# Joining 16-blocks of a batch element's triangular inverses in 64x64 tiles, two 32-blocks to a product, and a new order of all steps

## The chip, the cores and the metric

One Trainium2 chip, of which the kernel uses one core. The metric is device time in microseconds (us) from launch to end. The kernel before ran at a median of 657.1 us over 3 runs (648.14 to 662.64). Engines: PE is the matrix engine (products), PEld its loading of weights, DVE, ACT and POOL the vector, scalar and general engines, SP the engine that issues all DMAs here. Every fp32 product is shown in the profile as two records of a weight load and a matmul, so the counts of records are twice those of products.

## The reference, cut to what matters

```python
# q, k, v: (4, 8, 768, 48); beta: (4, 8, 768)
k_n = k / (norm(k) + 1e-6)
for t in range(768):
    y[:, :, t] = q[:, :, t] @ state
    v_old = state^T k_n[t]
    state = state + beta[t] * outer(k_n[t], v[t] - v_old)
x = y with the 8 heads side by side: (4, 768, 384)
h = relu(x^T @ w_tok1) @ w_tok2          # tokens mixed: 768 -> 256 -> 768
u = x + h^T
out = u + relu(u @ w_ch1) @ w_ch2        # channels mixed: 384 -> 1536 -> 384
```

## The kernel before, in words

The recurrence over 768 tokens is done in chunks of 64 tokens. A unit u is a pair of chunks (128 tokens) of one batch element with all 8 heads; there are 24 units, six to an element. For each of 16 (chunk, head) blocks of a unit the kernel forms the strictly triangular 64x64 matrix of products of keys, and needs the inverse of one plus that matrix. With the inverses there, a chunk is one step of a chain over chunks: the state is multiplied with the chunk's keys and queries (`p_k`, `p_y`), the rest of the values with the inverse (`p_w`), and the state is updated (`p_s`).

All engines take their instructions in program order. The program is a set of Python generators ("jobs"), each cut into steps by `yield`, and a string written out in the source, `order` (lines 1124 to 1193), names which job does its next step; every engine and the DMA queue on SP gets its instructions in that order. The jobs:

- `k<u>` loads keys and queries, `v<u>` values (line 406), `w<j>` one piece of the weights (`round_weights`, line 262): step 0 is the DMA on SP (line 271), step 1 two ACT passes (277, 278), step 2 a DVE pass (280), step 3 a POOL pass (284). The buffer of a piece, `d64`, has three copies, so the DMA of a piece waits for step 3 of the piece three before it in the order.
- `p<u>` prepares a unit: transposes of keys and queries (463, 481), products `p_g` (501), masked copies by DVE (507), and then `to_parts` (567): for the six units of the first element the four 32x32 diagonal blocks go to the tile `spare` by copies of ACT (572), DVE (575) and POOL (577); later units go by DMA to DRAM (584).
- `i<r>` inverts the 32x32 blocks of a round of units in DVE (`invert`, 615). The first element has the rounds 0 (units 0 to 3) and 1 (units 4, 5). For these two the elimination (637, 642) inverts two 16x16 diagonal blocks of each 32-block side by side in 14 steps, and step 15 writes a transposed copy `t16` of the upper 16 rows (651). Step 16 transposes the inverses back (654).
- `h<u>` (`join_16`, 661), first element only, fills the 16x16 off-diagonal block of each 32-block: per (chunk, head) block and per quarter of 32 partitions, one product with the 32-block as weights and 16 columns of `t16` (672), an ACT copy that keeps the lower 16 rows by a scale `low16` (675), one product of that with the 16 right columns of the 32-block (682), and four ACT copies into place (687). A unit has 32 products of each kind: 8 pairs of blocks times 4 quarters.
- `f<u>` (589) brings the inverted 32-blocks back, `j<u>` (694) joins two 32-blocks to a 64-block (`p_z` 715, `p_x` 718 and 734).
- `r<t>` (740) is the chain over the 48 chunks, 12 to an element. `m<b>` (943) is the whole mixer of element b: token mixing (950, 963), then the channel mixing (1030 or 922, then 1052). Its first `p_h` (963) needs all 12 chunks of its element.
- `x`, `z` (221) and `Y` (230) are fillers: products of zeros into a tile `p_warm` that nobody reads. `x` is a 128x128 product with 128 columns, `z` one with 512 columns (both line 225), `Y` four of 64x64 with 128 columns (235).

Tiles in PSUM of the names `p_z`, `p_x` and `p_g` share two buffers, tag "prep".

Of the kernel before, what the change touches and what calls it, by code (L numbers as in the profile page):

```python
# [23 lines left out]
def kernel(  # L24
# [402 lines left out]
    def gm_of(u):  # L427
        return gms[place(u)]
# [113 lines left out]
    )  # L542

# [71 lines left out]
    def invert(rnd):  # L615
# [45 lines left out]
    def join_16(u):  # L661
# [4 lines left out]
        bs = slice(j * NB, j * NB + NB)  # L666
        z = z16[:, bs]
        p_z = ps_prep([128, NB, QB], "p_z")
        for nb in range(NB):
            for i, (block, _, _) in enumerate(quarters(u)):  # L670
                r = slice(HB * i, HB * i + HB)
                nc.tensor.matmul(p_z[r, nb], block[:, nb], t16[r, :, j * NB + nb])
        taken_16.add(u)
        yield
        nc.scalar.activation(z, p_z, ACTF.Copy, scale=low16)
        yield
        assert inverted.issuperset((u, i) for i in range(4))
        p_x = ps_prep([128, NB, QB], "p_x")
        for nb in range(NB):
            for i, (block, _, _) in enumerate(quarters(u)):  # L680
                r = slice(HB * i, HB * i + HB)
                nc.tensor.matmul(
                    p_x[HB * i : HB * i + QB, nb], z[r, nb], block[:, nb, QB:HB]
                )
# [440 lines left out]
    x z w10 b*2 w10 k1 k0 k1*5 k0*2 w2 w1 w10*2 p1*2 k3 k0*3 z p0 p1 b p0*3 p1*2 p0*6  # L1125
    w2 p0 k2 p0 w1 k3 w2 w3 k3 p0 k2 k4*2 k3 p1*4 w1 p1 w1 p1 k4*2 k2 x k3 p0 z p1 p0
    k4 p1 k5*2 k2*3 p2*2 v0*2 w3*3 p2 k3 p3 p2 p3 p2*4 k5 p2*2 p3 p4 w13 p1 w18 z w2 p0
    p3*2 v0 p2 p3 v1 p2*2 p3*3 k5*2 k6 p2 p3 p4 k4 p3*3 p4 w13 w6 p2*2 p1*2 p3*2 k5 p4
    w13 k7*2 p3 i0*6 p5 i0*2 w6 p4*3 k6 p4 i0*4 k6 p4*2 i0*2 k6 i0 p4 w18 k6 z w18*2 i0
    p4*3 p5*2 v1 w13 Y h1*2 h0 i0 k7*2 p6*2 f0*2 w8 w17 f0 h2 h0*2 w8 f1 p5 k7 h0*2 p6  # L1130
    h0*2 h2 p5 v0 w17 f1*2 p7 w8*2 z k8 p4 w6*2 j0 f2 p5*3 k8 w17 f2 j0 h1 v0 j0 h1*3 z
    v1 h1 p7 j0*2 j1 f2 h2*2 w11 h2 z p5 x h2*2 p6 r0*2 p5 w17 r0 k8 w11 v1*2 w11 k8
    w11 r0 p5 p4 k7 w14*2 p5 k9 p5 w14 r0 k8 k9 p5 r1*2 j1 j2 j1 w14 k9*2 h3 f3 r1 p5
    r1 p5 i1 k6 h3 p6*2 Y w9*2 j1 r1 j2 r1 p6 r1 r2 z i1 f3 i1 w0 j1 k9 p8 r2 w0 z r2*2
    v2 j2 f3 h3 k9 r2 x h3 p6 h3*2 i1*4 k10 h3 p6 r2*2 w9 p6 i1 r3*2 i1 p7 w0 p6*3 v2*3
    k10*2 w0 k10 p7 r3 v2 w5 r3*4 j3 j2*2 p8 r4*2 j3*2 r4 v3 w9 r4 p7 i1 p7 i1 p8 p7
    w24 i1 p7*2 r4 k8 r4 p8 j3 i1 r5 i1 r5 j3 r4 i1 k10 p7 w5 p7 w5*2 p7 v3 r5*2 p7 p9
    v3*3 w16 r5*3 x r6 p6*2 w24 i1 v4 p8*2 v4 p8 w24*2 p6 r6 h5 i1 r6 h5 w27 w16 z h4
    r6 p7 h4 p8*2 p6 w16 w27 w16 p7 r6 f4*3 v4 p8*2 r6 w28 p9 p8*2 r7 w27*2 v4*2 h4 p9
    r6 p7 r7 p9 p7 w26 h4*4 p9*3 r7 p9 r7 p9 r7*2 w26*3 p8 w7 p9*4 j4 f5 p8 f5*2 v5 Y  # L1140
    p10 w28*2 z j4 p10 m0 w7*3 j4*2 r8*2 r7 j4 h5*2 p8*2 h5 p9*4 h5 r8*2 w28 z r8 j5 r8
    i2 w29 w15 x r9 k11 r8 w29 k11 i2*2 v5 h5 j5 i2 m0 r9 w29*2 i2*4 j5 v5 i2 r9 i2*3 x
    j5 r9 w15 r9*2 w15*2 j5 k11 w22 k11 v7 w22 v7 v5 p10 w4*2 r9 v7 w12 i2 z*3 i2*2 v5
    r10*2 i2 w4 m0 i2 p10 w4 i2 w12*3 m0 k10 k12*2 v7 w19 i2 r10*5 k12 i2 m0 i2 r11*2
    i2 w19*2 w21 i2 p10 r11 w22 k11 w19 k12 i2 w22 k12*3 v6 w25 v6 r11*2 i2*2 v6 p10
    r11 w31 i2*2 v6 k12*3 v6 p10 i2 p10*2 i2 k12 p10 m0 p10 m0 i2*2 m0 w25 m0 k11 f6
    p11*2 f6*3 m0*2 w21 f7*4 p10 m0*3 f8 w27 p10 w25 m0 w31 k12 p12*2 w31 f8*2 j6 w31
    p11 m0 p11 w23 f8 j6*2 m0 p12 w21*2 w25 j7*3 w29*2 m0 f9*2 w32 p11 r12 j8 p11 p12
    w20 p11 r12 s m0 v7 r12 w25 r12 w23 p10*3 f9 r12 j8 r13 w23 p12 w23 j8 m0 p11 r13*3
    p11*2 w23 x w32 f9 v8 w30 w20 r13*2 k13 w32 w20 p10 r13 p11*3 w20 k13 r14*2 p12 k13  # L1150
    w32 p12 k13*3 m0*2 k13 w30 m0 k13 p11 w30*2 v8 k13 r14 k13*2 r14 p12*2 p11 k13 p12
    p13 r14 p12*3 m0 p12 p13 r14*2 m0 p13 w23 w25 p13 w33 v8*2 m0 j9 r15 p13 m0 w23 p13
    r15 w25 m0 p11 m0 r15 p13 r15 w33 m0*2 r15 p13*2 k14 w33 r15 k14 p13*2 w33 r16 m0
    r15 v8 k14*4 p12 w33 p11 r16 w27 w33 w31 m0 w27 w33 w29 w31*2 p13*2 j9 m0 p13*2 m0
    j9 k14 r16 j9 r16*3 k14 p14*2 r16 m0 r17*2 p14*3 m0*2 r17 i3 r17 i3*4 v10 m0 v10
    r17*3 i3*3 k15 m0 i3*2 v9 r18 i3*2 p14 m0 v10 k14 m0 i3 v9 i3 k15*4 v9 k15*3 m0*2
    k14 i3*9 k14 i3 k14 i3 p14 v9*2 m0*3 k15 r18 k15 p14 i3*6 m0*2 i3 v10 j9 k15 m0*4
    k15 m0*9 r18 p14*2 f11 r18*4 f10*2 p15*2 f12 v10 f12 f11 m0*2 p15*2 f10*2 f13 m0
    r19 p15 f12 f11 m0 f11 m0 r19 p14 f13 j10 f13 m0*2 r19 p15 j10 j11 r19*2 k16*8 m0*2
    r19 j10 j11 v11*3 r20 m0*2 r20 r19 j12 j11 r20 p15 k16 r20 m0 r20*2 p16*2 p15*3 k16  # L1160
    v11 p16*2 r21 r20 r21 m0 p15 r21 p16 r21 j12 p14 j12 k16*2 p14*2 k17*2 r21*3 m0 s
    k17*5 p16*2 r22 v11 m0 r22*3 p16 m0 k17*4 r22 s v12 s j13 s p16 r22 k17 p16 r22 r23
    p16*3 v12 r23 v12 p15*4 p17*3 p14 p17 m0 p17 r23 m0 p17*2 r23 m0*2 p16 r23 p17*3
    v12 p16 m0 p17*4 m0 s m0 s*3 p17 m0 f12 m0 j13 s*4 r23 m0*3 v12 m0 i4*5 m0 i4*2
    k18*8 m0 i4 j13 r24 m0 i4 m0*2 r24 f13 r24 k18 m0 i4*2 k18 i4 m0*2 p18 i4 k18 p18*2
    m0*2 i4 r24 i4*3 m0 i4*2 k18 p18 r25 p18 m1 v14 r24 v14*3 i4 r25 m1*2 i4 k19 i4
# [63 lines left out]
```

## Time and profile before

| What | Value |
|---|---|
| median of 3 runs | 657.1 us (648.14, 657.1, 662.64) |
| the profiled execution: span from the first to the last instruction | 657.4 us |
| PE busy in it | 621.6 us, 9504 matmul records |
| start of the first inverse (`i0`, line 629) | 30.80 us |
| first product of `h` (672), of `j` (715), of `r` (779) | 42.48, 52.45, 61.65 us |
| first `p_h` of element 0's mixer (963) | 145.83 us |
| DMA moved | 50.30 MB |

The profile shows one execution. Its own time is the span, 657.4 us, which lies 0.3 us above the median of the runs. "Busy" is the time in which an engine had at least one instruction in work, an idle time is put down to the instruction that released the engine ("<-"), and "issue" is a wait for nothing that the profile shows. PEclk is the clock granted to TensorE, 1 being full speed.

### The profile page before, as it was taken

How to read it: one execution, taken by the hardware profiler on the slowest of the kernel's cores; microseconds unless marked ns; L12 is line 12 of the kernel's file. 1: busy time of each engine (PE TensorE's matmuls, PEld its weight loads, DVE VectorE, ACT ScalarE, POOL GpSimd, SP SyncE). 2: the span in 40 equal slices, each digit the busy share in tenths (PEclk: the TensorE clock that was granted, in tenths of full speed). 3: DMA queues.
4: the chain of work that ended last, by engine and by line, in shares of the span. 5: the costliest groups of instructions: out<-in, count | busy, mean ns of one | idle time of the engine just before them, and what ended most of it. 6: DMA issues, size and time to landing. Idle time of an engine off the chain costs nothing.

```text
span 657.4 us, 22208 instructions
## 1 busy us (share of the span) xinstructions
PE 621.6 (95%) x9504; PEld 534.9 (81%) x9504; DVE 446.8 (68%) x1127; ACT 257.8 (39%) x623; POOL 107.9 (16%) x145
## 2 busy tenths in 40 slices
PE   7658988989999999999999999999999999999998
PEld 5446776656888998877988999868999986999997
DVE  3892666798689857898885988588835452472743
ACT  6836557545641333213642514124415150132240
POOL 1434245224420113000310101000100000000000
PEclk9965689989999999999999999999999999999999
DMA  9845344676553344424435303200210100000000
GB/s 188 172 91 133 83 115 109 164 176 158 124 124 75 93 94 96 111 67 94 96 72 129 70 31 82 66 16 15 42 35 3 31 3 0 25 1 25 1 25 24
DMA packets 135778, 50.30 MB, mean 77 GB/s; under 512 B 114656, under 2 KB 130144, under 8 KB 135680
## 3 DMA queue, kind: packets, MB, share of 16 engines
q1 hardware_dynamic: 135680, 48.89, 32.8%
q8 instruction: 74, 1.21, 0.8%
q14 instruction: 24, 0.20, 0.1%
HBM read 39.42 MB, written 9.44 MB: 74 GB/s over the span
## 4 chain that ended last, share of the span: by engine, by line
PE 82%; DVE 6%; ACT 3%; DMA 3%; issue 2%; SPq 2%; POOL 0%; DVEq 0%; POOLq 0%; ACTq 0%
PE p_o L1052 24%; PE p_r L922 19%; PE p_c L1030 7%; PE p_h L963 5%; PE p L950 4%; PE p_k L757 3%; PE p_g L501 3%; PE p_y L775 3%; PE p_s L791 2%; PE p_warm L225 2%; DVE x L642 2%; PE p_z L715 2%; PE p_w L779 1%; DVE sub L637 1%; PE p_y L792 1%
## 5 line engine op out<-in xcount | busy, mean ns | idle before, releaser
L1052 PE MATMUL p_o<-wc,r 128*128 128x192 f32 x720 | 128.1, 330 | 1.1 <-ACT u_t L977 0.6
L1052 PEld LDWEIGHTS p_o<-wc,r 128*128 128x128 f32 x720 | 116.5, 190 | 3.8 <-ACT u_t L977 1.1
L934 DVE TENSOR_TENSOR r<-r,p_r 128x512 f32<-128x512 f32 x90 | 59.8, 684 | 43.3 <-PE p_r L922 42.3
L981 DVE TENSOR_TENSOR xb<-xb,p_o 128x192 f32<-128x192 f32 x84 | 29.4, 350 | 61.7 <-PE p_o L1052 61.5
L931 ACT COPY r<-p_r 128x512 f32<-128x512 f32 x54 | 31.6, 585 | 97.6 <-PE p_r L922 84.0
L642 DVE TENSOR_TENSOR x<-x,sub 128x84 f32<-128x84 f32 (+24 forms) x178 | 61.4, 345 | 6.1
L637 DVE TENSOR_TENSOR sub<-x 128x84 f32<-128x84 f32 (+24 forms) x178 | 57.5, 323 | 6.7 <-DMA x<-n_dram 2.8
L1030 PE MATMUL p_c<-u_t,wc 128*128 128x256 f32 x216 | 50.8, 386 | 0.6 <-ACT u_t L977 0.6
L1052 PE MATMUL p_o<-wc,s 128*128 128x192 f32 x288 | 50.9, 330 | 0.3 <-DVE xb L981 0.3
L414 POOL TENSOR_TENSOR v_st<-v_st,nrm 128x384 f32<-128x384 f32 x24 | 20.7, 864 | 184.3 <-DMA v_st<-in_v_dram 82.2
L1052 PEld LDWEIGHTS p_o<-wc,s 128*128 128x128 f32 x288 | 46.7, 190 | 1.5 <-DVE xb L981 0.9
L1030 PEld LDWEIGHTS p_c<-u_t,wc 128*128 128x128 f32 x216 | 39.8, 190 | 6.5 <-ACT u_t L977 0.9
L938 ACT ACTIVATE r<-r 128x512 f32<-128x512 f32 x54 | 33.9, 631 | 24.4 <-DVE r L934 24.0
L806 ACT ACTIVATE xb<-p_y 64x192 f32<-64x192 f32 x96 | 31.1, 324 | 26.1 <-PE p_y L792 9.8
L473 POOL TENSOR_TENSOR mb<-mask_c,cs 128x512 f32<-128x512 f32 x20 | 21.0, 1048 | 114.8 <-DVE cs L453 77.7
L922 PE MATMUL p_r<-u_t,wc 128*128 128x128 f32 x288 | 38.5, 277 | 0.0
L922 PE MATMUL p_r<-t_d,wc 128*128 128x128 f32 x288 | 37.3, 280 | 0.0
L922 PEld LDWEIGHTS p_r<-u_t,wc 128*128 128x128 f32 x288 | 35.3, 192 | 0.3
L783 ACT COPY w_t<-p_w 128x192 f32<-128x192 f32 x48 | 15.2, 317 | 51.8 <-PE p_w L779 51.3
L922 PEld LDWEIGHTS p_r<-t_d,wc 128*128 128x128 f32 x288 | 34.0, 191 | 0.9
L950 PE MATMUL p<-xb,w 128*128 128x384 f32 x96 | 34.4, 508 | 0.2 <-ACT xb L806 0.2
L284 POOL TENSOR_TENSOR wc<-w_f,d 128x384 uint32<-128x384 uint32 x24 | 25.0, 1042 | 57.9 <-ACT d L278 16.4
(171 smaller groups left out, 1212.2 us busy)
## 6 DMA issues: line engine op xcount, KB each, us to landing
d<-in_moe_w_ch_dram SPq DMA_DIRECT2D x24, 384.0 KB, 3.9
v_st<-in_v_dram SPq DMA_DIRECT2D x96, 48.0 KB, 2.5
out_dram<-xb SPq DMA_DIRECT2D x23, 192.0 KB, 1.9
kst<-in_k_dram SPq DMA_DIRECT2D x64, 48.0 KB, 2.7
n_dram<-gm SPq DMA_DIRECT2D x72, 32.0 KB, 2.0
pads<-in_k_dram SPq DMA_DIRECT2D x24, 96.0 KB, 2.5
pads<-in_q_dram SPq DMA_DIRECT2D x24, 96.0 KB, 2.5
gm<-w_dram SPq DMA_DIRECT2D x72, 32.0 KB, 2.1
```

The lines of the kernel that those rows point to most:

```text
L637: nc.vector.tensor_tensor(out=tmp, in0=y[:, :, 0:s, s : s + 1].to_broadcast([n, k, s, w]), in1=y[:, :, s : s + 1, s + 1 : m].to_broadcast( ...
L642: nc.vector.tensor_tensor(out=y[:, :, 0:s, s + 1 : m], in0=y[:, :, 0:s, s + 1 : m], in1=tmp, op=ALU.add,)
L806: nc.scalar.mul(y[:, :, D * i : D * i + D], p_y[PAR[1 - i]], 1.0 if c else -1.0)
L922: nc.tensor.matmul(p[:, i], pieces[i // width][:, at : at + 128], f[f"u{n}"], start=first and i == 0, stop=True, skip_group_check=True,)
L931: nc.scalar.copy(o, p)
L934: nc.vector.tensor_tensor(out=o, in0=o, in1=p, op=ALU.add if sign > 0 else ALU.subtract)
L938: nc.scalar.activation(o, o, ACTF.Relu)
L950: nc.tensor.matmul(p_1[dh], piece_of(w1, c, 0)[:, dh * 128 : (dh + 1) * 128], xb[:, c], start=(c == 0), stop=(c == NCH - 1),)
L963: nc.tensor.matmul(p_h, piece_of(w2, j, c * 128)[:, c * 128 : (c + 1) * 128], r1[j], start=(j == 0), stop=(j == NDH - 1),)
L981: nc.vector.tensor_tensor(out=xb[:, c, e], in0=xb[:, c, e], in1=p, op=ALU.add)
L1030: nc.tensor.matmul(p_c[:, k], piece_of(wc1, cb, f * 128)[:, f * 128 : (f + 1) * 128], u_t[:, cb], start=(cb == 0), stop=(cb == NCB - 1),)
L1052: nc.tensor.matmul(p, a[:, m], wc2[:, m, j], start=(start and i == 0), stop=(i == NM - 1), skip_group_check=True,)
```

## The change

For the first element's joins the four quarters of 32 partitions become two halves of 64, so that one product does two 32-blocks. The weights of the first product are the whole 64x64 matrix with two inverted 32-blocks on its diagonal, and its other operand is `t16` twice, once with the odd 32-blocks set to zero and once with the even ones. The result is copied with a scale that keeps the lower 16 rows of the even block, and again for the odd block, into a wider zeroed tile `z16`; the second product takes 48 columns of it as weights and 48 columns of the matrix. `z16` no longer lies in `spare` but in a buffer of the tag "xb", zeroed once by POOL at the first join. The count of products is 16 and 16 to a unit where it was 32 and 32.

```diff
-    for n in (QB * RU * NB, RU * NB * QB):
+    for n in (2 * QB * RU * NB,):
...
+    borrowed = {}
+
+    def z_of(u):
+        if not borrowed:
+            borrowed["z"] = mlp_pool.tile(
+                [128, NCH, NB * (C - QB)], FP32, name="z16", tag="xb"
+            )
+            nc.gpsimd.memset(borrowed["z"], 0.0)
+        return borrowed["z"][:, u].rearrange("s (b n) -> s b n", b=NB)
...
+    odd = const.tile([128, 1], FP32, name="odd")
+    nc.vector.tensor_scalar(
+        out=odd, in0=even, scalar1=-1.0, scalar2=1.0, op0=ALU.mult, op1=ALU.add
+    )
+    sides = const.tile([128, 2], FP32, name="sides")
+    for i, side in enumerate((even, odd)):
+        nc.vector.tensor_tensor(
+            out=sides[:, i : i + 1], in0=low16, in1=side, op=ALU.mult
+        )
...
-            nc.vector.transpose(t16, x[:, 0:QB])
+            nc.vector.transpose(t16[:, 0], x[:, 0:QB])
+            nc.scalar.activation(t16[:, 1], t16[:, 0], ACTF.Copy, scale=odd)
+            nc.vector.tensor_scalar(
+                out=t16[:, 0], in0=t16[:, 0], scalar1=even, scalar2=None, op0=ALU.mult
+            )
...
-        p_z = ps_prep([128, NB, QB], "p_z")
+        z = z_of(u)
+        wt = gm_of(u)[:, :, TC]
+        p_z = ps_prep([128, NB, 2, QB], "p_z")
         for nb in range(NB):
-            for i, (block, _, _) in enumerate(quarters(u)):
-                r = slice(HB * i, HB * i + HB)
-                nc.tensor.matmul(p_z[r, nb], block[:, nb], t16[r, :, j * NB + nb])
+            for r in PAR:
+                nc.tensor.matmul(p_z[r, nb], wt[r, nb], t16[r, :, :, j * NB + nb])
...
-        nc.scalar.activation(z, p_z, ACTF.Copy, scale=low16)
+        for i in range(2):
+            nc.scalar.activation(
+                z[:, :, HB * i : HB * i + QB], p_z[:, :, i], ACTF.Copy,
+                scale=sides[:, i : i + 1],
+            )
...
-        p_x = ps_prep([128, NB, QB], "p_x")
+        p_x = ps_prep([128, NB, C - QB], "p_x")
         for nb in range(NB):
-            for i, (block, _, _) in enumerate(quarters(u)):
-                r = slice(HB * i, HB * i + HB)
+            for r in PAR:
                 nc.tensor.matmul(
-                    p_x[HB * i : HB * i + QB, nb], z[r, nb], block[:, nb, QB:HB]
+                    p_x[r.start : r.stop - QB, nb], z[r, nb], wt[r, nb, QB:C]
                 )
...
-            nc.scalar.copy(block[0:QB, :, QB:HB], p_x[HB * i : HB * i + QB])
+            nc.scalar.copy(
+                block[0:QB, :, QB:HB],
+                p_x[HB * i : HB * i + QB, :, HB * (i % 2) : HB * (i % 2) + QB],
+            )
```

The string `order` is replaced as a whole. It names the same steps of every job as often as before, except the fillers: `x` 8 times before and once after, `z` 16 and 6, `Y` 3 and 2. The stretch up to the first chunk of the chain (`r0`), before:

```
x z w10 b*2 w10 k1 k0 k1*5 k0*2 w2 w1 w10*2 p1*2 k3 k0*3 z p0 p1 b p0*3 p1*2 p0*6
w2 p0 k2 p0 w1 k3 w2 w3 k3 p0 k2 k4*2 k3 p1*4 w1 p1 w1 p1 k4*2 k2 x k3 p0 z p1 p0
k4 p1 k5*2 k2*3 p2*2 v0*2 w3*3 p2 k3 p3 p2 p3 p2*4 k5 p2*2 p3 p4 w13 p1 w18 z w2 p0
p3*2 v0 p2 p3 v1 p2*2 p3*3 k5*2 k6 p2 p3 p4 k4 p3*3 p4 w13 w6 p2*2 p1*2 p3*2 k5 p4
w13 k7*2 p3 i0*6 p5 i0*2 w6 p4*3 k6 p4 i0*4 k6 p4*2 i0*2 k6 i0 p4 w18 k6 z w18*2 i0
p4*3 p5*2 v1 w13 Y h1*2 h0 i0 k7*2 p6*2 f0*2 w8 w17 f0 h2 h0*2 w8 f1 p5 k7 h0*2 p6
h0*2 h2 p5 v0 w17 f1*2 p7 w8*2 z k8 p4 w6*2 j0 f2 p5*3 k8 w17 f2 j0 h1 v0 j0 h1*3 z
v1 h1 p7 j0*2 j1 f2 h2*2 w11 h2 z p5 x h2*2 p6 r0*2 ...
```

and after:

```
b*2 w1 k0 w1 k1 k0*5 p0*2 k1 k2 k3 k1*4 k3 b z p1*2 w1*2 w10 w8 p0*8 p1*2 v1*2
p1*2 p0*3 v0 k2*5 p1*3 p2*2 p1*4 k4*3 w18 k3*4 p2*3 p3*2 p2*2 k4*2 p2*6 p3*3
p0*2 p3 p0 p3*3 k5 w10*3 p3*4 p4*2 p2 p1*2 v1 p2*2 k6 p1 k6 p3*3 i0 k4 v0 i0
w13 p4 w8 p4*2 k8 p4*2 k5*2 i0 w18*2 w13 k7*2 p4 i0*9 p4*3 k5*3 p4 z i0 v0 i0
k6 k7 p5 z v1 w18 i0*2 Y p4*2 v0*2 z*3 h1*2 w8*2 v1 w3*2 i0 k8*2 h0*2 f0*3 h2*2
p4*2 f1*3 p5*4 k6*2 h0*4 j0 h1 h0 f2 j0 p5 w3 p5*2 p6 j0*2 w3 h1*3 f2 p6 f2 w13
h1 w13 w24*2 j1 j0 p5 h2 k7*2 h2*3 r0*3 ...
```

More of the change, by code (lines that the diff above doesn't have):

```diff
@@ L1131 @@
[L1131 to L1154, printed above, removed]
@@ new lines @@
+    p4*2 f1*3 p5*4 k6*2 h0*4 j0 h1 h0 f2 j0 p5 w3 p5*2 p6 j0*2 w3 h1*3 f2 p6 f2 w13
+    h1 w13 w24*2 j1 j0 p5 h2 k7*2 h2*3 r0*3 w24 r0 r1 p7*2 w14*2 w24 r0 k9 h2 k8*2
+    r1 w6*2 w14 p6 p5 w14 p5 r1*2 p5*2 w2*4 j1*2 k6 w6*2 p5 r1*3 v2 j2 h3 f3*3 v2*2
+    h3 r2*2 p6 p5*2 j1*2 p6 v2*2 w11*2 i1*3 r2 i1 p6 w11 p8*2 p6 j2*2 r2 w16*4 w9
+    h3*5 r2*3 w9 p6*2 i1*2 k7 k10 r3*3 k9*4 w9 j3 p7*2 i1 p6*3 r3*3 k9 p8 p9 r3 w11
+    j2 p6 j2 r4 i1*2 w27*2 v3*3 j3*2 v3 k8 r4*3 p7 p8 p7*5 i1*3 r4*2 w5*3 j3*2 r5
@@ new lines @@
+    p7 i1*2 k10 r4 k10 w9 r5*3 w7*2 w5 v4 w27 i1 p7*2 r5 i1 p8 r5 p8*3 v3 p8 r5
+    r6*2 h5 r6 h5 r6 k10 p7*2 k10 h4*2 w27 w26*2 p9*2 k10 w7*2 p10 w0 i1 f4*2 r6*3
+    p8*4 r7 p6*2 p9*2 p6*2 f4 h4 r7*2 w28 v4 p9*3 w0*3 h4*3 j4 r7*2 p9*2 v4*2 h4 p9
+    w26*2 r7 w28*2 r8 w28 p8*4 r7 p9*2 p7*2 f5*3 j4*2 k11 p10 v4 r8 p10 m0 p10 v5
+    w17*2 j4 w17 h5 j4 r8 w17 Y r8 w29*2 r8*2 w29 p9*4 h5*4 j5 r8 r9*2 w4*3 m0 r9*2
+    i2*6 w12 i2 j5*2 w4 r9*2 k11*3 r9 w12 w29 v5 k12 x v5*3 p10*3 i2*3 w12*2 j5 i2
@@ new lines @@
+    r10 p10*2 r10 m0 j5 r10 i2*2 w19*4 p10*2 i2 k12*3 r10*4 m0 w15*2 k12*3 i2*2
+    r11*5 k12*2 k11 i2 v6 r11 w15*2 i2*4 v6 w31 v7 v6*3 w31 m0*2 w23 i2*2 k11 i2*2
+    m0 i2*3 k12 v7 k12*2 i2 v7*2 m0 i2*2 w23 i2 m0*2 w22 m0 p10*3 f6*4 m0*3 f7*3
+    w23*2 p11*8 s w22 p11 j6 w22 m0*3 f8 p11 p12*2 s*2 p12 j6 j7 p10 w27 w30 w22
+    w23 j6 m0 f8 j7*2 f8 j8 m0 r12*3 w31*2 f8 r12 w21*2 f7 j8 r13 w21*2 w27 w32 r13
+    w30 j8 p10 w30*2 p12*2 w23 r12 w31 m0 w20 r13*2 w32 r13*3 w25 k13*4 w31 v8*2
+    w32 w27 w20*2 v7 w25 v8 w20 w32 p11*3 k13*4 r14*2 p12*2 m0*3 p11*4 w29 p12
```

88 lines of the change are left out of this document (40 added, 48 removed).

## The prediction

> **What bounds the kernel now.** First the page's totals and slices, then busy time by stage (start, length, then PE, PEld, DVE, ACT, POOL busy, clock, DMA share, GB/s), for the dependence on time.
>
> ```profile
> PE 621.6 (95%) x9504; PEld 534.9 (81%) x9504; DVE 446.8 (68%) x1127; ACT 257.8 (39%) x623; POOL 107.9 (16%) x145
> PEclk9965689989999999999999999999999999999999
> ```
> ```profile
> 0.00:30.80 30.80, 23.16 (x228) 16.35 (x228) 18.10 (x52) 22.55 (x57) 7.91 (x19) 1.00 0.99 181
> 42.50:61.65 19.15, 15.04 (x464) 10.23 (x464) 9.86 (x18) 12.54 (x35) 9.74 (x13) 0.50 0.74 176
> 61.65:78.40 16.75, 16.31 (x352) 13.41 (x352) 9.72 (x24) 9.46 (x23) 5.81 (x7) 0.50 0.35 81
> 78.40:105.50 27.10, 23.10 (x800) 19.07 (x798) 16.12 (x47) 16.89 (x47) 10.78 (x14) 0.94 0.46 110
> 122.00:145.80 23.80, 19.79 (x308) 12.02 (x306) 22.60 (x57) 12.04 (x32) 7.51 (x9) 0.93 0.67 157
> 145.80:330.00 184.20, 183.22 (x2952) 155.21 (x2949) 149.85 (x372) 69.80 (x178) 40.71 (x49) 1.00 0.45 104
> ```
>
> After 145.8 us, the first p_h, PE is busy nearly without a gap: the end is that moment plus a fixed amount of PE work, so the change acts through what lies ahead of 145.8. There the bound moves: DMA (share 0.99) to 30.8, the inverse on DVE to 42.5, then PE at half clock to 78.4, then a mix, then DVE (22.60 of 23.80) from 122. Next, the chain of waits from 55 to 146, by line and its long pieces, and PE's timeline:
>
> ```profile
> 54.06 2.00 PE p_warm L225 x2
> 59.29 2.43 PE p_warm L225 x4
> 75.83 3.21 PE p_warm L225 x4
> 116.41 4.95 DMA d<-in_moe_w_ch_dram
> ```
> ```profile
> 46.50 0.29 PE L682 MATMUL p_x<-wc,r 32*16 32x16 f32 x13 [1.08 <-ACT r L675]
> 48.31 0.61 PE L682 MATMUL p_x<-wc,r 32*16 32x16 f32 x51 [1.52 <-issue]
> 59.11 0.18 PE L682 MATMUL p_x<-gm,r 32*16 32x16 f32 x1 [1.51 <-issue]
> ```
>
> Fillers lie on the chain, and the joins' small products show gaps for which nothing is to blame. Last, PE's groups by form and two waits:
>
> ```profile
> L757 PE MATMUL p_k<-s_t,kq 48*64 48x48 f32 x656 | 28.2, 226 | 2.3 <-DVE s_t L801 1.9 <-issue 0.3
> L715 PE MATMUL p_z<-t,gm 32*32 32x32 f32 x704 | 16.4, 195 | 0.4 <-DVE t L701 0.4
> L672 PE MATMUL p_z<-r,gm 32*32 32x16 f32 x256 | 3.7, 198 | 0.0
> L682 PE MATMUL p_x<-gm,r 32*16 32x16 f32 x256 | 3.2, 178 | 1.9 <-issue 1.5 <-DVE gm L507 0.4
> ```
> ```profile
> SPq L271 <- POOL wc L284: 16.9, 7, 6.0
> ACT d L277 <- DMA d<-in_moe_w_ch_dram: 11.4, 6, 2.8
> ```
>
> **The joins' products.** Busy time over records: 14.5 ns (L672) and 12.5 (L682), so 64 records of each make 0.93 + 0.80 = 1.73 us a unit. The new ones are 32 + 32 records with wider operands: between L715 (23.3 ns: 32 weight columns, 32 streamed) and L757 (43 ns: 64 weight columns, 48 streamed, on two halves of the array), 1.5 to 2.75 us. I take 2.4, nearer to L757, whose tile they share: +0.7 a unit, +4 us of PE over six units (-1.4 to +6). Half as many products are not cheaper ones.
>
> **To the first inverse** (30.80). DMAs count in SP's order. Before, unit 3's keys and queries are complete after 2,144 and 2,336 KB (summing line 242, 271, 383, 401 issues), after: 1,504 and 1,696; unit 2's queries at 2,784 and 2,800. At 181 GB/s the 640 KB are 3.5 us. ACT's work ahead of the last block copy (L572) falls from 22 to 19 us by its rows (three weight pieces move behind it). I take -3.4; ends 0 (unit 2's queries decide) and -5.
>
> **Inside the inverse.** Added on DVE's path: `cs` of unit 4 (0.24), one `gm` pass (0.66), and the masks: an ACT copy of 128x512 (L931 0.585, L938 0.631) that DVE waits for, then a DVE scale in place (0.4 to 0.72 by L280 and L473; 0.5), with two handovers of 0.1. But unit 4's `gm` now goes ahead of `t16`; before, the first p_z waited for it (42.48, while the transpose ended at 41.85). Sum 0.9 + 1.3 - 0.6 = +1.6. The POOL memset, 4.5 times L551's 0.526, is 2.4 us beside DVE's inverse; without that cover it would delay `w8` by as much. Three small DVE constants (about 0.2 each) fall into DVE's 2.6 us of idling before its first weight pass, or cost 0.6 there. The borrowed buffer is next wanted by element 1's output at chunk 12, long after the joins have read it: no wait.
>
> **First products to `j0`.** Here is the new wait. The DMA of piece `w3` is issued right after `w8`'s POOL step, whose buffer it takes, and its ACT passes right after the DMA in ACT's queue; `w8`'s DVE step lies behind the masks. Counting: first product 40.7, mask and `gm` done 41.3, `w8` DVE 41.7, POOL 42.7, SP, landing after 3.7 (page, 256 KB) 46.5, ACT 47.4. Behind it wait h0's z, now two copies (2 x 0.366; +2.2 us over six units), f0, h2's z, f1: x of h0 is in place at 51.9, t11 52.5, j0's product 52.5, as before (52.45). So +1.8 eats the lead. Ends: 0 (w3 lands unseen) and +4.
>
> **`j0` to the first chunk.** Before 52.45 to 61.65, 9.2 us, with fillers of 2.00 and 2.43 and a gap of 1.51. After, product 0.9, zst 0.75, product 0.8, ACT's copies for h1 1.04, `w24` 1.1 and j0's 0.72: 4.7 us, -4.4, and `r0` at 57.2. Late next is ACT. Ends: -2.5, -5.5.
>
> **`r0` to p_h** (84.2 us). Fillers on the chain: 1.05 + 3.21 + 0.42 + 0.63 + 0.70 = 6.0 off. The joins of units 3 to 5 add 2.1 on PE, half of it on the path: +1. Most weight pieces now have DMA and ACT step adjacent in the order (w24, w14, w6, w2, w11, w16, w27, w5, w7, w26), and w27, w7 and w26 their buffer freed just ahead; before such waits of 1.1 to 2.8 us summed to 14. Take +2 on the path (0 to +8). The clock: I counted the columns that PE streams per window of 3.41 us, weighted by the share of the array. Full clock was granted after windows of 1,322 to 1,644, lost after 926 to 1,104. From 98.9 to 129.6 us, four windows (1,452, 1,872, 2,064, 2,102) hold fillers of 1,024 to 1,536 and would fall below 900. Four more half-clock windows at 1.0 us each (p_k's 16 records take 0.66 us or 1.04; PE is about half of the chain) are +4; ends 0 and +24. DVE's work from `r8` to p_h, by rows, falls from 25.9 to 25.3: -0.6. Sum +0.4.
>
> **After p_h.** Counted by rows, the PE work left is 450 us in both orders; 0, ends -3 (all idle gone; PE is idle 7 us of 511) and +8.
>
> Sum: -3.4 + 1.6 + 1.8 - 4.4 + 0.4 + 0 = -4.0 from 657.4 gives 653.4 us; the profiled execution lies 0.3 over the median.
>
> [...] The gaps of 1.5 us before L682 follow 16,384-byte fetches on the instruction queue, with 508 and 1,526 PE instructions between the three of them (46.8, 57.6, 90.2). [...]
> The clock was 0.50 from 61.65 to 78.40 while PE was busy 16.31 of 16.75 us. [...]
>
> **The rivals.** (1) Slower: without fillers the half clock lasts through `r0` to p_h. For it: the clock stays at 0.50 over 37 us despite five fillers. Against: p_g and p_t windows are dense. From 78.4 on PE is busy 58 us, 9 of them fillers; 49 us at 1.6 times (p_k) to 2 times (p_g, 0.9 to 1.95) are 78 to 98 in 67 us of room: 653.4 - 4 + 11 to 31 = 660 to 680, 667 taken. It turns the sign from about eight half-clock windows on.
> [...]
> (3) The new order opens waits in the full stage, as before at 330 to 355 (PE 23.0 busy of 25): four such places, +8, 661.
> (4) The joins turn out on L715's side and `w3` lands unseen: -2.5 and -1.8, 649; part of the forecast's range.
>
> **Numbers.** Forecast with (4) 0.52, its own range 646 to 659; (1) 0.17, (2) 0.16, (3) 0.15. Two per cent is 13 us, about what a measurement of this kernel can tell from no change. Faster by that (below 644): 0.17, from (2) and a little of the forecast; slower (above 670): 0.10, the upper half of (1); same 0.73. The range 641 to 667 leaves out the ends of (1) and (2).
>
> **What would show it.** The first line-629 transpose near 27.4; an ACT wait of about 4 us for `w3`'s DMA near 42 to 46; line 779 first near 57; p_z and p_x records of 25 to 45 ns each; clock slices below 9 between 78 and 140; p_h near 142. I am wrong if p_h moves and the end doesn't, or if the clock stays full after 45 us.

## The result, and the profile after

| | Before | After |
|---|---|---|
| median | 657.5 us (4 runs, 648.14 to 662.64) | 680.0 us (4 runs, 677.21 to 682.3) |
| span of the profiled execution | 657.4 us | 679.2 us |
| first inverse (line 629, now 647) | 30.80 | 26.92 |
| first product of `h` (672, now 693) | 42.48 | 43.07 |
| first product of `j` (715, now 742) | 52.45 | 52.36 |
| first `r0` product (779, now 806) | 61.65 | 57.13 |
| first p_h (963, now 990) | 145.83 | 145.60 |
| from there to the end of the span | 511.6 | 533.6 |

The kernel after is slower: 1.048 times the time before, interval 1.040 to 1.056. It misses the forecast of 653.4 us and lies above the range, which ended at 667. The table says where: `r0` comes 4.5 us earlier, as forecast, p_h does not, and behind p_h, where the prediction had put nothing, 22 us are lost.

The page of the kernel after, totals and granted clock:

```profile
PE 627.7 (92%) x9078; PEld 549.6 (81%) x9078; DVE 458.4 (67%) x1132; ACT 259.9 (38%) x631; POOL 109.5 (16%) x146
PEclk9876678789979998999979999999999999999999
```

Its busy times by stage, with the columns of the table in the prediction; the last row is the one to look at:

```profile
43.07:57.13 14.06, 12.48 (x265) 11.53 (x265) 7.95 (x16) 10.78 (x30) 7.97 (x11) 0.62 0.32 81
57.13:78.40 21.27, 18.93 (x430) 17.27 (x426) 12.68 (x31) 17.65 (x49) 10.33 (x13) 0.56 0.65 165
78.40:105.50 27.10, 22.18 (x582) 20.61 (x584) 18.22 (x47) 15.11 (x41) 9.32 (x11) 0.71 0.48 112
122.00:145.60 23.60, 20.34 (x347) 13.80 (x344) 21.86 (x52) 10.53 (x27) 9.19 (x11) 0.82 0.59 140
145.60:330.00 184.40, 172.93 (x2576) 144.00 (x2576) 142.02 (x354) 60.03 (x157) 34.51 (x41) 0.97 0.41 95
```

From p_h to 330 us PE was busy 183.22 of 184.20 us before; now it is busy 172.93 of 184.40, and does 2,576 records where it did 2,952. So it is no longer PE alone that bounds this stage. Whom PE waits for there (145.6 to 460 us; engine, line, releaser: us, times, longest):

```profile
PE p_w L806 <- DVE rest L789: 5.4, 5, 2.5
PE p_k L784 <- DVE s_t L828: 4.0, 2, 2.8
```

The same two waits before (145.8 to 460 us):

```profile
PE p_k L757 <- DVE s_t L801: 0.7, 1, 0.7
PE p_w L779 <- DVE rest L762: 0.3, 1, 0.3
```

Both are steps of the chain `r` that VectorE (DVE in the views) does in its own order. What VectorE did ahead of the largest gap (PE idle from 190.5 to 193.3):

```profile
188.22 1.12 DVE L366 STREAM_TRANSPOSE kq<-pads 128x512 f32<-128x512 f32 x1 [2.10 <-DMA gm<-w_dram]
189.20 0.33 DVE L280 TENSOR_SCALAR w_f<-d 128x384 uint32<-128x384 uint32 x1
189.47 0.53 DVE L1031 TENSOR_TENSOR s<-r 128x384 f32<-128x384 f32 x1
190.03 1.25 DVE L1031 TENSOR_TENSOR s<-s,r 128x384 f32<-128x384 f32 x1
191.21 1.18 DVE L1031 TENSOR_TENSOR r<-r 128x384 f32<-128x384 f32 x1
...
192.84 0.34 DVE L828 TENSOR_TENSOR s_t<-s_t,p_s 128x192 f32<-128x192 f32 x1
```

VectorE stands 2.10 us for a DMA ahead of transposing the queries of unit 13. The line names a transfer that SP issued behind these rows, but the first of those landed at 188.58 us by the trace, when the transposing had begun. The last of the rows left SP at 183.90 and landed at 188.04, and VectorE's wait for its semaphore ended at 188.08: it was the load. VectorE then works off what is queued behind, the update of the state last, and PE needs that update. Two of the passes in between take 1.25 and 1.18 us; in a run below, in which GpSimd's passes only write zeros, the same two take 0.56 and 0.55. GpSimd (POOL) beside them:

```profile
189.67 1.20 POOL L284 TENSOR_TENSOR wc<-w_f,d 128x384 uint32<-128x384 uint32 x1 [3.65 <-DMA pads<-in_k_dram]
190.83 1.14 POOL L490 TENSOR_TENSOR gm<-kst,cs 128x384 f32<-128x384 f32 x1
```

So the load opens this gap of 2.8 us, and GpSimd makes it some 1.3 us longer, an estimate from these four times. How late the loads come shows also in the wait of ScalarE (ACT) for the loaded keys over 145 to 460 us, first after, then before:

```profile
ACT ksq L440 <- DMA kst<-in_k_dram: 32.2, 7, 7.9
```
```profile
ACT ksq L440 <- DMA kst<-in_k_dram: 12.9, 8, 5.4
```

### The profile page after: what moved, and what is told of

Same layout as the page of the kernel before. It is cut to its first block, busy times and chain, and to the rows that moved or that the text cites. A ratio compares the mean times of both kernels' runs of the same rounds, so it can differ in the third digit from the quotient of the medians.

```text
span 679.2 us, 21366 instructions
## 1 busy us (share of the span) xinstructions
PE 627.7 (92%) x9078; PEld 549.6 (81%) x9078; DVE 458.4 (67%) x1132; ACT 259.9 (38%) x631; POOL 109.5 (16%) x146
## 4 chain that ended last, share of the span: by engine, by line
PE 52%; DVE 18%; DMA 5%; SPq 4%; issue 3%; ACT 3%; POOL 1%; DVEq 0%; POOLq 0%; ACTq 0%
PE p_o L1079 18%; PE p_r L949 17%; DVE sub L655 5%; DVE x L660 5%; PE p_c L1057 4%; PE p_k L784 2%; SPq L627 2%; PE p_h L990 2%; PE p_s L818 1%; SPq L401 1%; DVE gm L507 1%; PE p L977 1%; PE p_y L802 1%; PE p_w L806 1%; DMA x<-n_dram 1%
## 5 line engine op out<-in xcount | busy, mean ns | idle before, releaser
L1079 PEld LDWEIGHTS p_o<-wc,r 128*128 128x128 f32 x720 | 118.4, 192 | 2.6 <-ACT u_t L1004 1.1
L660 DVE TENSOR_TENSOR x<-x,sub 128x84 f32<-128x84 f32 (+24 forms) x178 | 68.1, 383 | 6.1
L655 DVE TENSOR_TENSOR sub<-x 128x84 f32<-128x84 f32 (+24 forms) x178 | 61.5, 346 | 8.3 <-DMA x<-n_dram 4.0
L1079 PE MATMUL p_o<-wc,s 128*128 128x192 f32 x288 | 51.1, 330 | 0.3 <-DVE xb L1008 0.3
L806 PE MATMUL p_w<-rest,gm 64*64 64x48 f32 x656 | 30.4, 233 | 12.4 <-DVE rest L789 7.8
L949 PE MATMUL p_r<-t_d,wc 128*128 128x128 f32 x288 | 39.3, 289 | 0.0
L977 PE MATMUL p<-xb,w 128*128 128x384 f32 x96 | 36.8, 530 | 0.0
L949 PEld LDWEIGHTS p_r<-t_d,wc 128*128 128x128 f32 x288 | 35.7, 199 | 0.9
L806 PEld LDWEIGHTS p_w<-rest,gm 64*64 64x64 f32 x656 | 25.1, 144 | 13.8 <-DVE rest L789 5.0
```

The costliest lines, as they stand in the source:

```text
L655: nc.vector.tensor_tensor(out=tmp, in0=y[:, :, 0:s, s : s + 1].to_broadcast([n, k, s, w]), in1=y[:, :, s : s + 1, s + 1 : m].to_broadcast( ...
L660: nc.vector.tensor_tensor(out=y[:, :, 0:s, s + 1 : m], in0=y[:, :, 0:s, s + 1 : m], in1=tmp, op=ALU.add,)
L806: nc.tensor.matmul(p_w[r, p], gm[r, 2 * p + cc, TC], rest[r, p])
L949: nc.tensor.matmul(p[:, i], pieces[i // width][:, at : at + 128], f[f"u{n}"], start=first and i == 0, stop=True, skip_group_check=True,)
L977: nc.tensor.matmul(p_1[dh], piece_of(w1, c, 0)[:, dh * 128 : (dh + 1) * 128], xb[:, c], start=(c == 0), stop=(c == NCH - 1),)
L1079: nc.tensor.matmul(p, a[:, m], wc2[:, m, j], start=(start and i == 0), stop=(i == NM - 1), skip_group_check=True,)
```

## The experiments

Each ratio is against the kernel before, run on the same chip between the same runs. A table of the main ones first, with two numbers from each profile: when p_h begins, and how long the span goes on from there. The kernel before runs with a spread of its own (its medians in these groups lie between 649.8 and 654.6), and its profiled execution of 657.4 us is a late one, so the ratio decides, and the profile says where.

| Kernel | ratio (interval) | p_h | from p_h to the end |
|---|---|---|---|
| before | 1 | 145.8 | 511.6 |
| after | 1.048 (1.040, 1.056) | 145.6 | 533.6 |
| new joins, old order | 1.011 (1.004, 1.018) | 143.6 | 511.7 |
| old joins, new order | 1.036 (1.030, 1.042) | 137.2 | 531.5 |
| new up to 168 us, then old order | 1.020 (1.016, 1.025) | 144.2 | 520.8 |
| old up to 168 us, then new order | 1.035 (1.031, 1.039) | 147.7 | 525.6 |
| before without fillers behind `r0` | 1.004 (1.000, 1.008) | 138.9 | 511.3 |
| old joins, new order up to p_h | 1.009 (1.005, 1.013) | 144.0 | 513.4 |
| after, loads left out | 1.018 (1.012, 1.023) | 146.0 | 517.4 |
| before, loads left out | 0.994 (0.990, 0.998) | 140.5 | 509.4 |
| after, GpSimd's four passes zeroed | 1.012 (1.001, 1.023) | 129.8 | 525.1 |
| before, GpSimd's four passes zeroed | 1.001 (0.996, 1.006) | 133.8 | 513.7 |
| after, both | 0.995 (0.990, 1.000) | 129.6 | 514.6 |

**Joins or order.** The first four take the change apart: one string `order` under the other code, and the two strings cut at the last step of the last weight piece, near 168 us, and crossed. The edit of the first:

```diff
-    b*2 w1 k0 w1 k1 k0*5 p0*2 k1 k2 k3 k1*4 k3 b z p1*2 w1*2 w10 w8 p0*8 p1*2 v1*2
+    x z w10 b*2 w10 k1 k0 k1*5 k0*2 w2 w1 w10*2 p1*2 k3 k0*3 z p0 p1 b p0*3 p1*2 p0*6
...
```

and one of the seams, that of the third:

```diff
-    r16 m0*2 w23 j9 r16 w25 r16 p12 j9*2 r16
+    r16 m0*2 w23 j9 r16 w25 p12*3 p13 j9 r16*4
```

> The changed joins of the first element in the order of before, fillers included. Theory A (the loss of 22 us lies in the new order, in the stage after 168 us): 655 to 663, near before. Theory B (the wide joins, their masks and copies cost it): 675 to 682. Theory C (missing fillers ahead of the first p_h): 655 to 663.

> The joins of before in the new order. Theory A and C: 674 to 682, all of the loss without the new joins. Theory B: 655 to 662.

> The changed kernel with the new order up to the last step of a weight piece (about 168 us), then the steps left in the order of before, without fillers. Theory A: 655 to 664, since the stage after 168 us has the old order. Theory C: 674 to 682. Theory B: 675 to 682.

> The changed kernel with the order of before, its fillers included, up to the last step of a weight piece (about 168 us), then the steps left in the new order. Theory A: 672 to 682, with PE gaps of 1 to 3 us after 180 us and half-clock windows behind them. Theory C: 655 to 663. Theory B: 675 to 682.

Measured 657.0, 676.1, 664.6 and 674.4 us. The joins alone cost 1.1%, the order alone 3.6%: together the whole. Theories B and C fall as main causes. Of the order, the part behind 168 us costs most, but the part ahead of it is not free: with it, and the old order behind it, the gap at 190 us stays (2.37 us).

**Repairing it by hand.** The late steps were moved by a few places. The stretch around the gap at 190 us, as an example:

```diff
-    r15*2 f9*2 m0 p13 f9 r15 k14 r15 p13*2 k14 w33*3 k14 m0*5 w31 r15*3 p13*3 k14*3 p13
+    r15*2 f9*2 m0 p13 k14 f9 k14 r15 k14 r15 p13 k14*3 w33*3 k14 m0*5 w31 r15*3 p13*3 k14 p13*2
```

> The kernel after, with only some late steps of its order moved by 3 to 24 places: the loads of units 13, 14, 16, 17 and 20 (k13, k14, k16, k17, k20), and the steps f15 to f17 that bring inverses back, go earlier; p13's transposing of queries, which waits for such a load on VectorE, goes behind r15's update of the state, r21's first steps go ahead of p16's sum, and p14, p17, p20 somewhat later. Theory A (the loss after 168 us is a DMA that SP issues late, for which VectorE waits in its order with the chain's own step queued behind, each such gap followed by half clock): the gaps at 190, 257 and 340 us (2.8, 1.8, 2.5 us) shrink below 1 us, the half clock of 17 us behind them goes, and the time falls from 680 to 660 to 670. Rival D (SP is late because it issues without pause, so that an earlier place in the order moves nothing): gaps stay or move elsewhere, 676 to 684.

A clear miss: 701.7 us, ratio 1.076 (1.069 to 1.083). The moves opened other waits, the largest a gap of 5.5 us on PE at 294, where VectorE waits for a block that an earlier step now stored later:

```profile
DVE sub L655 <- DMA x<-n_dram: 6.3, 1, 6.3
```

The three gaps stayed as well (2.45 us at 193, 1.58 at 254, 2.74 at 345), as rival D had it. Since several things moved at once, this decides nothing between the two; it says much about how tightly these queues hang together. The next one left all waits and only put fillers into the gaps:

```diff
-    p13*3 k14*3 p13 j9 r16 k14*2
+    p13*3 k14*3 p13 j9 z*2 r16 k14*2
...
```

> The kernel after, with five fillers z more: two ahead of r16's first step, one ahead of r21's third, two ahead of r29's third, the steps that ended the gaps of 2.8, 1.8 and 2.5 us. The waits themselves stay. Theory A (a gap of two microseconds in the full stage costs as much again, since 3.4 to 6.8 us of half clock follow it): the half clock behind 190, 257 and 340 us (17 us in all) goes, and with it 6 to 8 us: 671 to 675. Rival E (the half clock there costs nothing much, or comes for another reason): 678 to 684, the half clock stays or the fillers' own 5 us come on top.

678.7 us, ratio 1.040 (1.034 to 1.046): a miss of theory A as it stood, and rival E's time. The half clock behind the three gaps did go (17 us of it, with 6.8 us new at 272), but the time hardly moved; at 270 PE now waits 2.5 us for the same transposed rows that it waited 1.2 us for in the kernel after, and VectorE works without a pause through both waits. So here the half clock is what a gap leaves behind, not what sets the time: a PE that is faster up to there waits longer for VectorE.

**A new head on the old code, and no fillers.**

The first joins the new string's first 875 steps (units 13's and 14's loads a few places earlier, as above) to the old one's rest; at the seam, with the new string's own continuation taken out, and a place of the second:

```diff
-    m0*2 w23 j9 r16 w25 r16 p12 j9*2 r16
+    m0 p14 m0 w23 j9 r16 w25 p12*3 p13 j9 r16*4
```
```diff
-    h3 p6*2 Y w9*2 j1
+    h3 p6*2 w9*2 j1
...
```

> The joins as before, the steps up to the last weight piece (875 steps, to about 168 us) in the new order with the moves of the run before that concern units 13 and 14 (the gap at 190 us), and from there the old order without its fillers. Theory A: p_h comes near 137, as with the new order and the old joins (137.15), 8 us ahead of before; without the gap at 190 that lead lasts to the end: 643 to 650, beside 652.8 of the kernel before. Rival D (the head leaves SP behind, whatever follows): the gap at 190 stays and the lead is gone, 652 to 660.

> The kernel before without its fifteen fillers behind r0 (8 z, 5 x, 2 Y); nothing else is changed. The prediction took 6.0 us of fillers off the chain between r0 and p_h and put 4 us of new half clock on it. Theory A (they about pay for themselves): half clock between r0 and p_h doubles from 23.5 to 35 to 50 us, p_h moves by less than 3 us, the time is 650 to 656. Rival C (the missing fillers are what made the new kernel slow): p_h later by 5 or more, 660 to 672. Rival F (fillers are mere ballast): p_h 6 us earlier, 645 to 648.

The first gave 666.7 us, 1.023 (1.015 to 1.030), p_h 138.1, with gaps of 3.2 us at 171 and 2.4 at 189: rival D, and worse than its 652 to 660. The head of the new order leaves transfers late here too: at 171 VectorE had stood 4.5 us for ScalarE, and ScalarE 4.1 us for the DMA of a weight piece. The second gave 653.9 beside 650.8, theory A's time: fifteen fillers behind `r0` are worth nothing that counts either way, with half clock between `r0` and p_h up from 23.5 us to 41. From `r0` to p_h it takes 84.0 us, where the kernel before took 84.2, so what the prediction balanced against each other here (6.0 us off, half clock on) does balance. That p_h comes 6.9 us earlier than in the profile before, where theory A had less than 3, lies ahead of `r0`, where the two programs are the same.

**Without the loads.** The decisive pair leaves the loads of keys and queries from unit 13 on out of both orders:

```diff
-                nc.sync.dma_start(
+                if u < 13:
+                    nc.sync.dma_start(
...
-                nc.sync.dma_start(
+                if u < 13 or src is v:
+                    nc.sync.dma_start(
```

> The kernel after, with the loads of keys and queries of units 13 to 23 left out (lines 357 and 401 for k; their steps issue nothing, and what reads them reads what an earlier unit left there). Order and everything else stay. Theory A (loads that SP issues late open the gaps after p_h): the gaps at 190, 257 and 340 us fall below 1 us, PE idles less than 6 us after 168 (15.5 in the kernel after), and the time falls to 657 to 664, 1.02 or less times the next kernel's. Rival G (it isn't the loads: the weight pieces, the inverses brought back, or simply the order on VectorE): the gaps stay, 672 to 680.

> The same left out of the kernel before: the control for the run above. Theory A: in the old order these loads are early enough, so that leaving them out gains less than 1%: 646 to 654. Rival G: the same. If instead it gains as much as in the new order (20 us), the loads cost the same in both orders and theory A falls.

663.8 and 647.7 us. In the new order this takes 3.0% off, in the old one 0.6%; the three gaps are gone, and so is the half clock behind them. PE's largest waits from p_h to 460 us in the first of the two:

```profile
PE p_z L745 <- DVE t L731: 2.6, 4, 0.9
PE p_k L787 <- DVE s_t L831: 1.8, 2, 1.2
PE p_w L809 <- DVE rest L792: 1.1, 3, 0.4
```

So theory A is right for the larger part of what is lost behind p_h: 16.2 of 22 us by the table, or 14.0 if the 2.2 that the control gains there are taken off. It isn't met in full: PE still idles 7.2 us behind 168 us (less than 6 expected), and the two kernels stand 1.024 apart, not 1.02. And the run takes the loads' issues off SP with the loads. The gap at 340 us, where VectorE stood 3.3 us for inverses brought back and not for a load, went too. So the pair shows what the late loads and their place on SP cost together.

**What the joins cost.** `t16` laid out so that a product streams neighbouring columns, in the old order:

```diff
-    t16 = spare[:, cuts[1] : cuts[2]].rearrange("s (q t b) -> s q t b", q=2, t=QB)
+    t16 = spare[:, cuts[1] : cuts[2]].rearrange("s (b q t) -> s q t b", q=2, t=QB)
```

> The new joins in the old order, as in the first experiment, with t16 laid out so that the 16 columns that a product streams lie next to each other (they lay 32 floats apart). Theory S (p_z's 58 ns a record, against 40 of p_x with half as many columns again, come from reading scattered columns): p_z's 192 records fall from 11.2 us to 6 to 8, the time stays within 1% of the 657.0 of the first experiment. Rival T (two products side by side instead of four, each with twice the columns, cost four times 14.5 ns whatever the layout): 58 ns stay.

658.3 us, 1.010 (1.006 to 1.015), a second measure of the joins. The layout changes nothing: the 192 records of p_z take 10.5 us here and 10.5 in the first experiment, which has the same order and the old layout (the 11.2 us of the expectation are the kernel after's). Theory S falls. By form, in the kernel after:

```profile
L693 PE MATMUL p_z<-r,gm 64*64 64x32 f32 x128 | 7.6, 290 | 0.0
L706 PE MATMUL p_x<-gm,z 64*48 64x48 f32 x128 | 4.9, 243 | 0.4 <-ACT wc L711 0.4
L693 PE MATMUL p_z<-r,wc 64*64 64x32 f32 x64 | 3.6, 291 | 4.5 <-DVE r L671 4.5
L706 PE MATMUL p_x<-wc,z 64*48 64x48 f32 x64 | 2.8, 278 | 0.0
```

18.9 us for 384 records, where 768 took 10.6 before. The 58 ns a record of p_z against 14.5 before mix two clocks: in the kernel after all six units' p_z ran at a granted clock of 0.50, before two of the six ran at 1.00. Where a unit's p_z stands alone, its 32 records take 1.89 us at 0.50 (kernel after) and 1.14 at 1.00 (first experiment); the old 64 took 1.13 and 0.74. That is 3.3 and 3.1 times as much a record, with half as many records. p_x, by the same count, takes 1.52 and 0.92 us where it took 0.94 and 0.69. That two products run beside each other and not four is how the tiles lie in the code; that this sets the cost, as rival T has it, is argued and not shown.

**A short head.** The old joins with the first 632 steps of the new order, the old one behind them; the new string's continuation at the seam and what stands there now:

```diff
-    i2*4 v6 w31 v7 v6*3 w31 m0*2 w23
+    i2*4 v6 w31 v7 v6 w22*2 v7*3 m0 i2 w21
```

> The joins as before; the first 632 steps in the new order, to just ahead of the first p_h, and then the old order without its fillers. Theory A (the new order's head is good for some microseconds up to p_h and its loss begins behind it): no gap near 190 above 1 us, p_h 137 to 140 as with the whole new order and old joins, and 642 to 650, a little below the kernel before. Rival H (the new head leaves loads and weight pieces behind that the rest must make up): gaps of 2 us and more between 145 and 200, 652 to 662.

657.4 us, 1.009: rival H by the time, though not by its gaps (one of 2.1 us, at 142). No combination of the two orders that was tried beats the kernel before.

**Why the loads are late.** Another queue for the loads, in both orders, and for the output stores that hold SP up:

```diff
-                nc.sync.dma_start(
+                (nc.sync if u < 13 else nc.gpsimd).dma_start(
...
-            nc.sync.dma_start(out=out[b, c * 128 : (c + 1) * 128, e], in_=xb[:, c, e])
+            nc.gpsimd.dma_start(out=out[b, c * 128 : (c + 1) * 128, e], in_=xb[:, c, e])
```

> The kernel after, with the loads of keys and queries of units 13 to 23 issued on GpSimd's DMA queue and no longer on SP's. Nothing is left out and the order is the same; a load now waits only for GpSimd's steps ahead of it and for its buffer. Theory Q (the loads are late because SP issues them behind other transfers that wait, such as 28 us of output stores waiting for xb): most of the gain of leaving them out comes, 662 to 668. Theory P (they are late because their buffers come free late: one pair of row tiles, refilled after VectorE's transposing, which the new order puts late): the gaps stay, 675 to 684, or the waits of GpSimd are new and it is slower still.

> The same change of queue in the kernel before, the control and a candidate. Leaving these loads out gained it 0.6%: theory Q 645 to 651, at best as good as the kernel before; theory P 648 to 658.

> The kernel after, with the output stores alone (line 1011) on GpSimd's queue; the loads stay on SP. SP waited 28.2 us for xb ahead of these stores between 160 and 370 us, 15.3 us in one piece. Theory Q: a part of the loads comes in time, 668 to 676; the gap at 190 us, ahead of the first store, stays. Theory P: 678 to 684.

681.6 us (1.043, 1.033 to 1.053), 670.4 (1.031, 1.019 to 1.043) and 685.9 (1.052, 1.044 to 1.060). The first lies in theory P's range; the other two are slower than either theory had it. Moving the stores gains nothing, and a queue of their own doesn't bring the loads in time, which speaks for theory P. There the loads stand and wait for their buffer, the one pair of row tiles that VectorE's transposing sets free (GpSimd's waits in the first, 145 to 460 us):

```profile
POOL pads L357 <- DVE kq L366: 54.2, 7, 19.8
```

It isn't clean: on GpSimd the loads hold up its own passes, and the control loses 3%: `rest` now waits 13.3 us for values that GpSimd scales late, where it waited 3.9 before (145 to 460 us). How much of the lateness is the buffer, and how much SP's own sequence, stays open.

**GpSimd beside the elimination.** In the stretch up to p_h the traces show something else. VectorE, then GpSimd, in the kernel after:

```profile
29.65 0.21 DVE L655 TENSOR_TENSOR sub<-x 128x52 f32<-128x52 f32 x1
29.89 1.10 DVE L660 TENSOR_TENSOR x<-x,sub 128x52 f32<-128x52 f32 x1
30.91 1.01 DVE L280 TENSOR_SCALAR w_f<-d 128x384 uint32<-128x384 uint32 x1
31.84 0.22 DVE L655 TENSOR_TENSOR sub<-x 128x72 f32<-128x72 f32 x1
32.10 1.06 DVE L660 TENSOR_TENSOR x<-x,sub 128x72 f32<-128x72 f32 x1
```
```profile
29.88 1.04 POOL L473 TENSOR_TENSOR mb<-mask_c,cs 128x512 f32<-128x512 f32 x1 [3.47 <-DVE sub L655]
30.88 0.83 POOL L490 TENSOR_TENSOR gm<-kst,cs 128x384 f32<-128x384 f32 x1
32.06 1.01 POOL L284 TENSOR_TENSOR wc<-w_f,d 128x384 uint32<-128x384 uint32 x1 [0.35 <-issue]
```

The operation at 29.89 us takes 1.10 us, where the fastest of its shape takes 0.21. GpSimd starts a pass just ahead of it (29.88), and it ends just after that pass (30.99 against 30.92). Summed over the elimination's operations that take 0.15 us or more longer than the fastest of their shape: 6.8 us in 11 of them before, 17.5 us in 29 after (2.4 in the first inverse, 9.7 from `r0` to p_h, 5.4 behind it). The test replaces GpSimd's four reading passes by zeroing:

```diff
-        nc.gpsimd.tensor_tensor(out=dst.bitcast(U32), in0=f, in1=lo, op=ALU.add)
+        nc.gpsimd.memset(dst, 0.0)
...
-        scaler.tensor_tensor(
+        if u in EARLY_SC:
+            scaler.tensor_tensor(
...
+        else:
+            nc.gpsimd.memset(mb, 0.0)
```

> The kernel after, with GpSimd's four passes that read SBUF with two operands (lines 284, 414, 473, 490) replaced by zeroing the tile they write: GpSimd works for about as long, but reads nothing, and no longer waits for the operands; the sums that these passes form are left out. Theory L (a VectorE operation with two operands from SBUF stands still while GpSimd reads SBUF, and the new order puts more of GpSimd's passes beside the elimination): the elimination's operations, stretched by 17.5 us in all in the kernel after, are stretched by less than 3; the first inverse takes 13.5 us and not 16.15 to the first product, p_h comes 4 to 8 us earlier, and the time falls to 666 to 676. Rival M (the stretching comes from ScalarE or DMA writing beside it): 12 us or more of it stay, 676 to 682.

> The same in the kernel before, the control; its elimination was stretched by 6.8 us. Theory L: less than 2 us of that stay and the time is 644 to 651, so that the ratio of the two kernels falls by about a per cent. Rival M: the stretching stays and the time too.

657.9 and 649.3 us. No operation of the elimination is stretched any more, in either, though 28 of them still run beside a GpSimd pass in the new order. One of these, with the pass beside it:

```profile
75.67 0.27 DVE L663 TENSOR_TENSOR x<-x,sub 128x112 f32<-128x112 f32 x1
75.57 0.53 POOL L476 MEMSET mb<- 128x512 f32 x1 [9.00 <-DVE gm L510]
```

In the kernel after the same operation took 1.10 us beside the same pass of 1.04. VectorE's busy time, over the same number of instructions, falls by 23.9 us in the new order and by 13.6 in the old. Theory L, and worth more than expected: 3.5% in the new order, nothing in the old one, and p_h comes 15.8 us earlier in the new order, where 4 to 8 were expected. The test changes more than the reading, though. The passes did not stay about as long: GpSimd's busy time falls from 109.5 to 56.5 us, and its waits for operands go as well. That the stretching comes with the reading is shown; how much of the 3.5% it is, and how much the shorter passes, is not.

**Both.** The edits of the two pairs in one kernel, the new joins in the new order:

```diff
+                if u < 13:
+                    nc.sync.dma_start(
...
+        nc.gpsimd.memset(dst, 0.0)
...
```

> The kernel after with both things taken away: the loads of keys and queries of units 13 to 23 left out, and GpSimd's four reading passes replaced by zeroing (the sums are left out). Alone they took the ratio from 1.048 to 1.018 and to 1.012, while in the old order they changed it by -0.6% and +0.1%. If they are two separate causes, they add: 1.048 - 0.030 - 0.036 = 0.982, some 638 us, with p_h near 130 and no gap over 1.5 us behind it. If they are the same waits seen twice (a late GpSimd pass holding up the load that follows), the time stays near the better of the two, 652 to 660.

648.6 us, 0.995 (0.990 to 1.000), between the two expectations: of 3.0 and 3.5% together 5.3 are left, so they are mostly separate. The new order without both stands where the old one does without one or the other (0.994 and 1.001); the old one without both was not run. Behind p_h, 3.0 us of the 22.0 are left.

## Why the prediction was wrong, point by point

**To the first inverse:** 26.92 where 27.4 was said; right, though the old order's own profiles start it anywhere from 28.5 to 30.8 us.

**Inside the inverse:** mis-sized, +4.5 us (11.68 to 16.15) and not +1.6. The masks cost 1.28 as worked out (0.79 of waiting for ACT's copy, and the scale 0.49), `gm` 0.68. Missing were the 2.4 us by which GpSimd's passes stretch three operations of the elimination, and 0.65 by which one stretches a weight pass (1.01 for 0.36); of GpSimd's queue only the memset was looked at.

**First products to `j0`:** the wait for `w3` did not come. ACT takes the piece at 45.60, straight behind its z copies. This stretch took 9.29 us, 0.7 less than before, where 1.8 more were forecast, so that two errors cancelled and `j` began at 52.36 as "forecast". A date that comes true does not prove the terms behind it.

**`j0` to the first chunk:** 57.13, as said (-4.4).

**`r0` to p_h:** 88.5 us for 84.2, +4.3 and not +0.4. The fullness count foretold that the clock would fall without the fillers, but 50 us of half clock came and not 37. In both profiles the granted clock changes only after multiples of 3.41 us (before: 0.50 for 3.41 us from 92.05, for 6.83 from 30.61, for 37.55 from 40.85), and the windows were counted in that step. It was no clean threshold: with each record of the profile before counted where it starts, the window from 47.7 us holds 1,562 columns and half clock follows, where full clock follows the 1,322 of the one from 92.05; and of two with 1,120, the one from 51.1 is followed by half clock and the one from 85.2 by full. The joins' PE time rose by 8.3 us, beyond its upper end of 6: a unit's new products take 2.06 us at full clock, near the 2.4 that was taken, but 3.4 at half clock, and the term had no clock in it. And the elimination was stretched by 9.7 us, 4.6 more than before: at 84 us three stretched operations in a row hold `rest` back, and PE stands still for 2.0 us. The gaps of 1.5 us ahead of line 682 (the third of those counted, at 90.2, was one of 1.7 ahead of line 734) did not come back; the sum had no term for them, and needed none.

**After p_h:** the step that failed. "Counted by rows, the PE work left is 450 us in both orders", and so a term of 0 with an upper end of +8, is right in that PE's work is the same (6,862 records behind p_h before, 6,857 after) and says nothing on whether PE gets it in time. 22.0 us were lost here: PE's idle time behind 168 us rose from 3.6 to 15.5, with 17 us of half clock in the wake of its gaps. Rival (3) named the place and the kind and gave it 0.15 and 8 us; it had priced a wait by the only ones to be seen in the old order, and never set each late load's place on SP against its reader's place in the new one. The leads of the loads were counted up to the first inverse and no further. Of the 22.0, leaving out the late loads takes 16.2, zeroing GpSimd's passes 8.5, and both 19.0, so that the two overlap; the second of them, GpSimd beside VectorE, was in no rival. Rival (1) reached up to 680 us, but by half clock ahead of p_h, where the new order lost 4.3 us: the time alone would have spoken for it, the place does not.

**The baseline:** 657.4 us was a late execution. Without the late loads' lines the kernel before is the same program up to unit 13's load behind p_h, and in that profile the clock was half for 10.2 us from 41.1 and not for 37.5 from 40.8, `r0` came at 57.8 and p_h at 140.5. Against the median of some 650 us that the later runs gave, a forecast of 653.4 was no gain at all.

**The sum:** -3.9 +4.5 -0.7 -4.4 +4.3 +22.0 = +21.8, which is the difference of the spans.

## What to carry to other kernels

When a whole order of steps is replaced, PE's remaining work is no bound for the stage in which PE was full: for each load, compare its place on the issuing queue with its reader's place, and ask what the chain has queued behind that reader. Look at what GpSimd does beside VectorE's serial stretches as you look at VectorE's own queue. And fewer, larger products need not be cheaper: half as many, twice as wide, took 18.9 us of PE here where 10.6 had been.

## What the runs showed of the hardware that was not expected

In the kernel after, 29 operations of the elimination on VectorE took 0.62 to 1.12 us where the fastest of their shapes took 0.21 to 0.41. Beside each ran a GpSimd pass that reads SBUF, and each ended 0.07 to 0.27 us after that pass. With GpSimd's four passes zeroing, not one such case was left in the elimination. Zeroing itself did not stretch the elimination's two-operand operations (0.26 us beside the memset of 2.02 us in the kernel after).

The masks' scaling (line 671), with one operand from SBUF, took 2.35 us in the run with neighbouring columns and 2.96 in the new joins under the old order, there beside a reading pass (1.01 us from 40.53) and that memset behind it (2.02 us from 41.48). It took 0.49 in the kernel after, where GpSimd was idle. Whether either pass held it up no run here shows.

The kernel before, unchanged, ran anywhere from 642.6 to 662.6 us, the run of 642.6 at a mean granted clock of 0.984 and one of 658.4 at 0.955. One profile of it was no sure ground for terms of one or two microseconds.
